# Attention and mixture of experts on one core: transposes as 64-row tiles on two PSUM banks, products with v in four pieces, a new order of steps, one condition at the end

## The chip, the core and the metric

The kernel runs on one core of a Trainium2 chip. Its time is the device time in microseconds (us) of one execution: 1096.68 us, the median of three runs (1095.84 to 1097.83).

## What is computed

Attention with a bias that depends on position, then a mixture of experts with one expert per token (top 1). B = 8, 8 heads, 576 positions, 64 per head; 4608 tokens of width 512; 8 experts with an inner width of 1024.

```python
scores = scale * np.matmul(q, k.transpose(0, 1, 3, 2))
...                                    # bias[head, i, j] from positions, a small two-layer net
scores = scores + bias.transpose(2, 0, 1)[None, :, :, :]
attn = np.exp(scores - np.max(scores, axis=-1, keepdims=True))
attn = attn / (np.sum(attn, axis=-1, keepdims=True) + 1e-09)
attn_out = np.matmul(attn, v)
x = np.ascontiguousarray(attn_out.transpose(0, 2, 1, 3)).reshape(B * S, H * D)
logits = x @ w_gate + modality_bias[modality_id]
e_idx = np.argmax(logits, axis=1)
...                                    # gate_w: softmax of logits at e_idx
for e in range(E):
    mask = e_idx == e
    h = np.maximum(x[mask] @ w1[e], 0.0)
    out[mask] = gate_w[mask, None] * (h @ w2[e])
```

## The kernel before, in words

The kernel has four stretches: a setup (bias tables, first loads), attention, the MoE tiles, and a short end. All instructions are issued in the order in which the program writes them; no scheduler reorders them, and each engine works through its own queue.

**Attention** goes by pairs of heads, n = 0 to 31, four pairs (NP) a batch. A pair has 576 positions in five chunks of rows: 0 to 3 of 128 positions for each of the two heads, and chunk 4, which holds the last 64 positions of both heads side by side. Its steps, by the letter that they have in the table `ORDER` (L560), are:
- P: `prep` (L377) transposes q (P0), k (P1) and their last 64 positions (P2) on TensorE, with an identity as the other operand. H: `high` (ACT) rounds the result to fp32r, with q scaled; G: `low` (DVE) makes the difference from it. Scores are then three products: high by high, high by low, low by high.
- S0 to S4: `scores` (L401) multiplies a chunk of q with k in halves of 288 columns, the two heads on the two 64-row tiles of TensorE, into the banks `sps`; `biased` adds the bias and takes the minimum on DVE (L433). E0 to E4: `exps` (L447), exp with the sum of the row on ACT.
- T0 to T3: `etrans` (L459) transposes a chunk of the exponentials as 64-row tiles, upper rows into bank `eps0`, lower rows into `eps1`; t copies the two banks out. T4 takes chunk 4 as four full 128x128 transposes into one bank.
- C0 to C3: `compact` (L449) gathers on POOL columns 512 to 575 of the exponentials into `rem`; R: `rtrans` (L482) transposes these, four full transposes. C4: two POOL copies (L454) put chunk 4's last columns into the two diagonal blocks of `r4`; N: `rtrans4` (L491) multiplies `r4` by a doubled identity.
- A, B: `av` (L499), the product of the exponentials with v, in two pieces of 256 and 320 columns, the heads on two column tiles; a and b copy the pieces to `xTb`.
- L, V: loads of q, k and v. D, Z: a store and a scatter of routing, on SP and POOL. X, B (without n): one routing step of the batch before, from the lists of `route_steps`; the scatters `s_scatter` (L868) write token numbers into the table `tab` in DRAM, five a batch.

A plus or a minus in the table means the next or the previous pair. The five strings are five slots of a pair's time; `attention` (L568) runs them for n = 0 to 32.

**Routing** of a batch works beside the next batch's attention: logits (`s_logits`), their transposes, the choice of expert, ranks, positions in the table, and the token rows (`s_rows`), which are transposed by TensorE (25 full transposes a batch, logits included), scaled by POOL (L851) and stored.

**The MoE part** goes by tiles of 256 tokens of one expert. Five first tiles use what is known early, then tiles up to number 14 always run, and four more ran here under a condition each: `more` (L1319) loads column 3 of the table `tab_big` on every engine and skips the rest at zero. After them come two more conditions: `small`, tiles of 128 (`tab_small`), and `tiny`, tiles of 32 (`tab_tiny`). None of these had anything left to do here. The values are read by `values_load` in `reg` (L1080) and compared by each engine's queue.

Of the kernel before, what the change touches and what calls it, by code (L numbers as in the profile page):

```python
# [109 lines left out]
class Attn:  # L110
# [155 lines left out]
    def attn_early(self, st, rst):  # L266
# [29 lines left out]
        self.r4 = [cp.tile([P, P], F32, name=f"r4{k}") for k in range(2)]  # L296
        for t in self.r4:
            nc.gpsimd.memset(t, 0.0)
        self.id2 = cp.tile([P, 64], F32, name="id2")
        nc.vector.tensor_copy(self.id2[0:64, :], self.idf[0:64, 0:64])  # L300
        nc.vector.tensor_copy(self.id2[64:P, :], self.idf[64:P, 64:P])
        self.qraw, self.kraw, self.vmain, self.E, self.rem, self.sums, self.xT = {}, {}, {}, {}, {}, {}, {}

    def attn_late(self, st):
# [3 lines left out]
        self.eps = [pp.tile([P, 512], F32, name=f"eps{k}") for k in range(2)]  # L308

    def xbank(self):  # L310
        if "p2" in self.at:
            return self.ring("p2")
        self.n_x += 1
        return self.xps[self.n_x % 2]

    ON_ACT = ("av0", "av1", "e0", "e4", "xr", "lt0")

    def take(self, what, out, ps):

        if what in self.ON_ACT:  # L320
# [128 lines left out]
    def compact(self, n, c):  # L449

        if c == 4:
# [47 lines left out]
    def av(self, n, half):  # L499
# [19 lines left out]
        if half == 1:  # L519
            del self.vmain[n]  # L520
# [1038 lines left out]
```

## Time and profile before

| | |
|---|---|
| median of three runs | 1096.68 us (1095.84 to 1097.83) |
| the profiled execution | 1097.01 us, span of the trace 1095.2 us |
| busy share of the span | PE 94%, PEld (weight loads) 73%, DVE 68%, ACT 62%, POOL 21% |
| attention, steady part | 137.07 to 609.50 us |
| MoE tiles | 629.27 to 1081.40 us |
| after the last product | 1081.40 to 1095.20 us |

Times in the trace count from the start of the span. The profiled execution took 1.8 us more than its span and 0.33 us more than the median. In the rows, `PE` is TensorE's matmuls, `PEld` its weight loads, `PEldq` and `POOLq` the queues' own instructions (loads of values, branches). `L410` is line 410 of the kernel.

### The profile page before, as it was taken

What the parts mean: (1) busy time and instruction counts of PE and PEld (TensorE: products, weight loads), DVE (VectorE), ACT (ScalarE), POOL (GpSimd) and SP (SyncE); (2) the same over time, 40 slices, a digit from 0 to 9 for tenths busy, and PEclk for the clock granted to TensorE, in tenths of its full rate; (3) what the DMA queues carried; (4) which work ended last, traced back from release to release, by engine and by line L of the source; (5) the groups of instructions that cost most, each with busy time, mean ns of one, the idle gap of its engine ahead of it and who ended that gap; (6) DMA issues with size and microseconds to landing.
All of it is one profiled execution on the core that took longest, in us unless ns stands there. A gap on an engine that the chain in (4) does not pass through costs nothing. (4 is left out here: it accounts for less than half of the span.)

```text
span 1095.2 us, 25162 instructions
## 1 busy us (share of the span) xinstructions
PE 1028.3 (94%) x9502; PEld 800.6 (73%) x9502; DVE 739.5 (68%) x1641; ACT 681.5 (62%) x1351; POOL 232.4 (21%) x453
## 2 busy tenths in 40 slices
PE   6989999799999999999999899999999999999994
PEld 3447776566767667677666588889878799889994
DVE  7977778567777677877788466885545455564553
ACT  6767777657768677687776654555534455554552
POOL 0001212222313123142231422431111112111210
PEclk9999999989999999999999999999999999999998
DMA  6853222322322323233234401222545611111110
GB/s 167 213 146 71 66 56 54 74 60 53 90 66 80 65 55 76 71 84 71 53 88 132 122 21 49 59 73 76 182 159 207 206 40 59 39 49 40 64 44 26
DMA packets 125662, 93.29 MB, mean 85 GB/s; under 512 B 94738, under 2 KB 103314, under 8 KB 125525
## 3 DMA queue, kind: packets, MB, share of 16 engines
q1 hardware_dynamic: 117908, 71.20, 23.9%
q0 software_dynamic: 7520, 20.30, 6.1%
q8 instruction: 82, 1.34, 0.6%
q14 instruction: 56, 0.45, 0.2%
q10 hardware_dynamic: 96, 0.00, 0.0%
HBM read 141.40 MB, written 19.38 MB: 147 GB/s over the span
## 5 line engine op out<-in xcount | busy, mean ns | idle before, releaser
L447 ACT ACTIVATE Eb<-Eb,mn 128x576 f32<-128x576 f32 x288 | 221.1, 770 | 50.4 <-DVE mn L433 49.4
L433 DVE CUSTOM_DVE_ANT_0 Eb<-sps,NBm 128x576 f32<-128x576 f32 x256 | 183.5, 754 | 20.7 <-PE sps L410 15.3
L1180 PE MATMUL p<-QK,w1hi 128*128 128x256 f32 x1152 | 163.6, 285 | 1.5 <-ACT w1hi L1153 1.5
L1180 PEld LDWEIGHTS p<-QK,w1hi 128*128 128x128 f32 x1152 | 149.9, 193 | 8.9 <-issue 5.0
L410 PE MATMUL sps<-QK 64*128 64x288 f32 x1536 | 137.9, 309 | 4.7 <-DVE mn L433 4.1
L510 PE MATMUL xps<-eT,vraw 128*64 128x320 f32 (+1 forms) x1024 | 138.4, 412 | 0.0
L323 DVE COPY eT<-eps 128x512 f32<-128x512 f32 x128 | 87.8, 686 | 73.1 <-PE eps L473 73.0
L1183 DVE SCALAR_TENSOR_TENSOR hl<-p,hh 128x512 fp32r<-128x512 f32 x72 | 49.6, 689 | 121.4 <-ACT hh L1182 115.3
L321 ACT COPY eT<-eps 128x512 f32<-128x512 f32 x160 | 92.7, 580 | 53.0 <-PE eps L465 26.2
L1182 ACT ACTIVATE hh<-p 128x512 fp32r<-128x512 f32 x72 | 43.0, 597 | 125.7 <-PE p L1180 105.6
L410 PEld LDWEIGHTS sps<-QK 64*128 64x128 f32 x1536 | 110.3, 188 | 8.6 <-DVE mn L433 7.9
L510 PEld LDWEIGHTS xps<-eT,vraw 128*64 128x64 f32 x1024 | 67.9, 137 | 48.6 <-issue 6.1
L473 PEld LDWEIGHTS eps<-idf,Eb 64*128 64x128 f32 x2048 | 77.9, 139 | 32.9 <-ACT xTb L321 9.9
L1147 DVE TENSOR_TENSOR w2lo<-NBm,w2hi 128x1024 fp32r<-128x1024 f32 x72 | 89.3, 1240 | 15.1 <-ACT w2hi L1146 14.8
L473 PE MATMUL eps<-idf,Eb 64*128 64x64 f32 x2048 | 98.3, 231 | 1.0 <-ACT eT L321 0.6
L1206 POOL DMA_INDIRECT out<-mo,idt x36 | 36.2, 1004 | 296.5 <-ACT mo L1205 279.0
L457 POOL COPY rem<-Eb 128x128 f32<-128x128 f32 x128 | 36.8, 293 | 291.3 <-ACT Eb L447 289.1
L1180 PE MATMUL p<-QK,w1lo 128*128 128x256 f32 x576 | 93.6, 285 | 0.7 <-DVE w1lo L1154 0.7
L1147 DVE TENSOR_TENSOR w1lo<-NBm,w1hi 128x1024 fp32r<-128x1024 f32 x72 | 84.9, 1221 | 3.6 <-ACT w1hi L1146 1.0
L1180 PEld LDWEIGHTS p<-QK,w1lo 128*128 128x128 f32 x576 | 80.2, 194 | 1.1 <-DVE w1lo L1154 1.1
L1146 ACT CAST w2hi<-NBm 128x1024 fp32r<-128x1024 f32 x72 | 74.8, 1039 | 0.0
L1146 ACT CAST w1hi<-NBm 128x1024 fp32r<-128x1024 f32 x72 | 72.3, 1060 | 0.0
(241 smaller groups left out, 1763.2 us busy)
## 6 DMA issues: line engine op xcount, KB each, us to landing
NBm<-moe_w SPq DMA_DIRECT2D x20, 2048.0 KB
NBm<-moe_w SPq DMA_DIRECT2D x40, 1024.0 KB
NBm<-moe_w SPq DMA_DIRECT2D x32, 512.0 KB
NBm<-xTb SPq DMA_DIRECT2D x32, 288.0 KB
qraw<-q SPq DMA_DIRECT2D x64, 128.0 KB
kraw<-k SPq DMA_DIRECT2D x64, 128.0 KB
vraw<-v SPq DMA_DIRECT2D x32, 256.0 KB
xg<-xrb SPq DMA_DIRECT2D x28, 258.0 KB
```

The costliest lines, as they stand in the source:

```text
L321: self.nc.scalar.copy(out, ps)
L323: self.nc.vector.tensor_copy(out, ps)
L410: nc.tensor.matmul(self.sps[h or 0][:, half, 0:HS], QD[:, a, :] if h is None else QK[o, 0, a, P * c : P * c + P], QK[o, 1, b, ks], start=i ...
L433: nc.vector.tensor_tensor_reduce(out=e.rearrange("p (t w) -> p t w", t=2), in0=ps, in1=nb.rearrange("p (t w) -> p t w", t=2), scale=1.0, s ...
L447: self.nc.scalar.activation(e, e, AF.Exp, bias=mn, scale=-1.0, accum_out=sm)
L473: nc.tensor.transpose(self.eps[r][:, w : w + 64], e[o, h, P * k : P * k + P], self.idf[o, o])
L510: nc.tensor.matmul(ps[o, :], v[:, h, k, :] if k < 4 else self.vrem[n % 2][:, o], eT[:, h, k, sl] if k < 4 else rT[:, sl], start=k == 0, st ...
L1146: self.nc.scalar.copy(h, w)
L1147: self.nc.vector.tensor_tensor(l, w, h.bitcast(F32), op=ALU.subtract)
L1180: nc.tensor.matmul(ps[:, a, :], w[:, c, fs], x[:, c, :], start=i == 0, stop=i == len(ops) - 1)
L1182: nc.scalar.activation(hh[:, sl, :], ps, AF.Relu)
L1183: nc.vector.scalar_tensor_tensor(hl[:, sl, :], ps, 0.0, hh[:, sl, :].bitcast(F32), op0=ALU.max, op1=ALU.subtract)
```

## The change

Transposes. A new helper `turn` transposes 128 rows as two 64-row tiles: rows 0 to 63 into bank 0, rows 64 to 127 into bank 1 of a pair of banks (`e` = `eps`, `x` = `xps`). The transposes of q, k and their remainders, of chunk 4, of the remainder columns, and of routing's logits and token rows use it, and every result is copied out as two halves, one per bank. N multiplies E directly, on two column tiles, without `r4` and the copies of C4. GpSimd scales q in advance (`scale_q`, 128x512 in place), so `high` and `low` of q need no scale.

Products with v. `av` works in four pieces of 128, 144, 160 and 144 columns, each in an `eps` bank of its own.

Order. The table becomes the one below, a pair's work reaches two pairs on, and loops go to n_pair + 2. After the colon stands the pair of banks or the bank (`:e`, `:x`, `:e0`) or the engine of a copy (`:a` ACT, `:v` DVE); x and y copy a routing step's result out, O is a routing step without TensorE's banks. E now stands for one head's exp at a time.

End. The big table gets a column 4, which says whether any work of any kind is left. Each conditional tile is preceded by that condition and then by its own; small and tiny lie inside the last of them.

```diff
-        self.r4 = [cp.tile([P, P], F32, name=f"r4{k}") for k in range(2)]
...
+    def turn(self, ps, col, x, idf=None):
+
+        for r in range(2):
+            o = slice(64 * r, 64 * r + 64)
+            n = x.shape[1]
+            self.nc.tensor.transpose(ps[r][0:n, col : col + 64], x[o, :], self.idf[o, o])
...
+    def scale_q(self, n):
+
+        x = self.qraw[n].rearrange("p c h d -> p (c h d)")
+        self.nc.gpsimd.tensor_scalar(x, x, self.SC, None, op0=ALU.mult)
...
-                nc.tensor.transpose(ps[:, j, :], x[:, j, :, :].rearrange("p h d -> p (h d)"), self.idf)
...
+                self.turn(bk, 64 * j, x[:, j, :, :].rearrange("p h d -> p (h d)"))
+            hi, lo = (QK[:, part, a, 0:512].rearrange("p (j r w) -> p j r w", j=4, r=2) for a in range(2))
+            return [
+                (bk[r][:, 0:256].rearrange("p (j w) -> p j w", j=4), hi[:, :, r], lo[:, :, r], 1.0) for r in range(2)
+            ]
...
-                self.nc.gpsimd.tensor_copy(self.r4[n % 2][o, o], self.E[n, 4][o, 0, 512:S])
...
+                for k in range(4):
+                    self.nc.tensor.transpose(bk[h][:, 64 * k : 64 * k + 64], e[o, 0, P * k : P * k + P], self.idf[o, o])
...
+        for c in range(4):
+            self.turn(bk, 256 + 64 * c, self.rem.pop((n, c)).rearrange("p h w -> p (h w)"))
...
-        self.nc.tensor.matmul(ps, self.r4[n % 2], self.id2, start=True, stop=True)
...
+            self.nc.tensor.matmul(
+                ps[o, :],
+                self.E[n, 4][:, 0, 512:S],
+                self.idf[:, o],
+                start=True,
+                stop=True,
+                tile_position=(0, 64 * h),
...
-    CUT = 256
...
+    CUT = (0, 128, 272, 432, S)
...
+        sl = slice(self.CUT[part], self.CUT[part + 1])
+        ps = self.banks[u[0]][int(u[1])][:, 0 : sl.stop - sl.start]
...
     ORDER = (
-        "T2- t2- S0 T4- N- t4- R- P0+ E0 n- r- C0 D",
-        "T3- t3- S1 H0+ G0+ A- E1 L++ C1 a- X B Z",
-        "T0 t0 S2 P2+ P1+ H2+ G2+ H1+ E2 S4 G1+ X D E4 C4 C2 B",
-        "T1 t1 S3",
-        "B- E3 C3 b- X D V+ B Z",
+        "T2-:e t2- S0 Q+ A2--:e0 a2--:a Y:e1 y X:x E0 T3-:e",
+        "x t3- S1 A3--:e0 N-:e1 E0 E1 n- D E1 a3--:v T4-:x R-:x T0:e C0 C1 Z r-:a O",
+        "t4-:a t0 S2 O A0-:e1 a0-:a E2 P2+:x E2 P0+:x",
+        "H2+ T1:e H0+ V t1 S3 E3 D C2 G0+ A1-:e1",
+        "L++ a1-:v E3 S4 P1+:x H1+ G1+ G2+ O Z C3 O E4",
     )
...
-        for n in range(n_pair + 1):
+        for n in range(n_pair + 2):
...
         def more(t):
-            if t < T:
-                with tc.If(self.reg("big", t - K, 3, mybir.ALL_ENGINES, 1) > 0):
+            with tc.If(self.reg("big", t - K, 4, every, 1) > 0):
+                if t == T:
+                    small(0)
+                    with tc.If(self.reg("tiny", NQ, 3, every, 1) > 0):
...
+                with tc.If(self.reg("big", t - K, 3, every, 1) > 0):
                     self.moe_load(t + 1)
                     self.tile(t)
-                    more(t + 1)
+                more(t + 1)
...
         more(self.sure)
-        small(0)
-        with tc.If(self.reg("tiny", NQ, 3, mybir.ALL_ENGINES, 1) > 0):
-            for _ in self.tiny(1):
-                pass
```

What moves, as the two programs have their instructions in their queues (line, operation, out<-in, shape; in brackets the queues and engines for whose semaphores a row waits).

TensorE, around the next pair's k, before: `kraw` is transposed (P1), then come S4 (`QK,QD`), T1, S3, a piece of the product with v, T2, and S0 (the scores that read the other `QK`).

```order
L386 MATMUL xps_77<-idf,kraw_1299 128x128 [waits DMAHW2_49,DMAHW1_49]
L386 MATMUL xps_77<-idf,kraw_1299 128x128 x3
L410 MATMUL sps_728<-QK_73,QD_109 128x288 [waits DVE_49]
L410 MATMUL sps_728<-QK_73,QD_109 128x288 x5
L473 MATMUL eps_730<-idf,Eb 128x64 [waits Activation_49]
...
L410 MATMUL sps_728<-QK_73 128x288 [waits DVE_49]
...
L510 MATMUL xps_78<-eT_105,vraw_1185 64x320 x8
L510 MATMUL xps_78<-rT,vrem_110 64x320 x2
L473 MATMUL eps_730<-idf,Eb 128x64 [waits Activation_49]
...
L410 MATMUL sps_728<-QK_72 128x288 [waits DVE_49]
L410 MATMUL sps_729<-QK_72 128x288 [waits DVE_49]
```

TensorE, the same place, after:

```order
L416 MATMUL sps_738<-QK_72,QD_108 128x288 [waits DVE_49]
L416 MATMUL sps_738<-QK_72,QD_108 128x288 x5
L322 MATMUL xps_77<-idf,kraw_1765 128x64 [waits DMAHW5_49,DMAHW4_49,DVE_49]
...
L322 MATMUL eps_740<-idf,Eb 128x64 [waits Activation_49]
L322 MATMUL eps_741<-idf,Eb 128x64 [waits DVE_49]
...
L416 MATMUL sps_738<-QK_73 128x288 [waits DVE_49,Activation_49]
...
L416 MATMUL sps_738<-QK_73 128x288 [waits DVE_49]
...
L528 MATMUL eps_740<-eT_106,vraw_1723 64x160 [waits Activation_49]
L528 MATMUL eps_740<-eT_106,vraw_1723 64x160 x7
L528 MATMUL eps_740<-rT,vrem_114 64x160 x2
L322 MATMUL eps_740<-idf,Eb 128x64 [waits Activation_49]
```

Now k's transposes follow S4, T2 alone stands between them and S0, and S0 waits for ACT and DVE at its first product, and for DVE at its third (shown) and ninth: high parts, low parts, low part of k's remainder. The third piece of the product with v is in `eps_740`, and T3 behind it waits for ACT to copy that bank out.

DVE between S4 and S0 after the change (L439 with `mn_8` is chunk 4's bias and minimum, with `mn_0` that of S0; L341 and L343 are low parts, L329 the copy t2):

```order
L439 ISA Eb,mn_8_3283<-sps_738,NBr 128x576 [waits DVE_49,PE_49,Pool_49]
...
L341 TENSOR_TENSOR QK_73<-xps_77,QK_73 128x4x64 [waits Activation_49]
L341 TENSOR_TENSOR QK_73<-xps_78,QK_73 128x4x64 [waits Activation_49]
L343 SCALAR_TENSOR_TENSOR QD_109<-xps_77,QD_109 128x64
L343 SCALAR_TENSOR_TENSOR QD_109<-xps_78,QD_109 128x64
L341 TENSOR_TENSOR QK_73<-xps_77,QK_73 128x64
L329 COPY eT_105<-eps_741 128x8x64 [waits PE_49]
L439 ISA Eb,mn_0_3335<-sps_738,NBm 128x576 [waits DVE_49,PE_49,Pool_49]
```

The low parts of k stand behind chunk 4's minimum, and ahead of the copy of T2.

POOL, around a scatter (L868, later L922, a DMA into `tab`), before:

```order
L868 DMA tab<-ids,pos_2532 36992x1 [waits DVE_49]
L851 TENSOR_TENSOR xrb_92<-xrb_92,rec 128x512 [waits Activation_49]
L854 COPY xrb_92<-gt_2403 128x4
L454 COPY r_119<-Eb 64x64 [waits Activation_49]
L454 COPY r_119<-Eb 64x64 [waits DMASW0_49,Pool_49]
L457 COPY rem_2_2603<-Eb 128x128 [waits PE_49,Pool_49]
```

and after:

```order
L458 COPY rem_2_3555<-Eb 128x128 [waits PE_49,Activation_49]
L922 DMA tab<-ids,pos_3161 36992x1 [waits DMASW1_49]
L458 COPY rem_3_3605<-Eb 128x128 [waits Activation_49]
L386 TENSOR_SCALAR qraw_3569<-qraw_3569 128x512 [waits DMAHW2_49,DMAHW1_49]
L798 COPY rec<-mv_3485 64x4 [waits DMAHW5_49]
L458 COPY rem_0_3763<-Eb 128x128 [waits Activation_49]
```

The copies into `r_118` and `r_119` (the two `r4`), one of which waited for a scatter's DMA queue, are gone; a scatter now waits for an earlier scatter, and the scaling of q (L386) has come to POOL.

## Rows read from the trace of the kernel before

**Rows 1.** Busy time by stretch: the stretch and its length in us, then the busy time of PE (its matmuls), PEld (its weight loads), DVE, ACT and POOL with the count of instructions, the granted clock of PE as a share of full speed, the busy share of the DMA engines, and GB/s. The stretches are attention from pair 4 to the last pair's chunk 4, the MoE tiles, and the end.

```profile
137.07:609.50 472.43, 442.14 (x5081) 322.03 (x5082) 350.53 (x992) 342.18 (x826) 117.02 (x292) 0.99 0.30 75
629.27:1081.40 452.13, 449.34 (x2919) 394.02 (x2919) 274.51 (x373) 227.35 (x300) 92.31 (x97) 1.00 0.26 84
1081.40:1095.20 13.80, 0.01 (x1) 0.00 (x0) 0.00 (x0) 0.69 (x1) 1.00 (x1) 0.63 0.09 29
```

**Rows 2.** PE's timeline at the starts of chunk 4's scores (step S4, once a pair): start and length in us, engine, line, operation, out<-in, tile and shape, count.

```profile
137.07 1.07 PE L410 MATMUL sps<-QK,QD 128*128 128x288 f32 x6
205.40 1.06 PE L410 MATMUL sps<-QK,QD 128*128 128x288 f32 x6
231.33 1.06 PE L410 MATMUL sps<-QK,QD 128*128 128x288 f32 x6
282.43 1.06 PE L410 MATMUL sps<-QK,QD 128*128 128x288 f32 x6
349.96 1.06 PE L410 MATMUL sps<-QK,QD 128*128 128x288 f32 x6
370.37 1.05 PE L410 MATMUL sps<-QK,QD 128*128 128x288 f32 x6
556.51 1.06 PE L410 MATMUL sps<-QK,QD 128*128 128x288 f32 x6
574.95 1.06 PE L410 MATMUL sps<-QK,QD 128*128 128x288 f32 x6
```

**Rows 3.** PE's timeline through one pair without routing beside it, same columns: k's transposes, S4, the second piece of the product with v, T2, S0, T4, N, R, P0, T3, and later the first piece and T0.

```profile
121.04 0.60 PE L386 MATMUL xps<-idf,kraw 128*128 128x128 f32 x4
121.66 1.06 PE L410 MATMUL sps<-QK,QD 128*128 128x288 f32 x6
...
124.66 2.38 PE L510 MATMUL xps<-eT,vraw 128*64 128x320 f32 x16
126.87 0.71 PE L510 MATMUL xps<-rT,vrem 128*64 128x320 f32 x4
127.50 0.71 PE L473 MATMUL eps<-idf,Eb 64*128 64x64 f32 x16
128.03 1.03 PE L410 MATMUL sps<-QK 64*128 64x288 f32 x12
128.99 0.66 PE L465 MATMUL eps<-idf,Eb 128*128 128x128 f32 x4
129.48 0.33 PE L494 MATMUL eps<-id,r 128*128 128x64 f32 x2
129.65 0.61 PE L488 MATMUL xps<-idf,rem 128*128 128x128 f32 x4
130.10 0.60 PE L386 MATMUL xps<-idf,qraw 128*128 128x128 f32 x4
130.63 0.89 PE L473 MATMUL eps<-idf,Eb 64*128 64x64 f32 x15
...
132.35 1.95 PE L510 MATMUL xps<-eT,vraw 128*64 128x256 f32 x16
134.13 0.60 PE L510 MATMUL xps<-rT,vrem 128*64 128x256 f32 x4
134.66 0.71 PE L473 MATMUL eps<-idf,Eb 64*128 64x64 f32 x16
```

**Rows 4.** Waits on the `r4` copies, by engine and line: what waited and for what, us in total, times, longest. The first row is PE's in the stretch 100 to 600 us, the second POOL's in the whole execution.

```profile
PE eps L494 <- POOL r L454: 12.0, 3, 7.8
...
POOL r L454 <- DMA tab<-ids,pos: 49.5, 17, 8.1
```

**Rows 5.** Groups of instructions by line and shape: engine, operation, out<-in with shapes, count, then busy us in total and mean ns of one, then idle time before them. The bias and minimum of the scores, the exp, the high and low parts of q and k in two sizes, one copy of a piece of the product with v, and the scaling of token rows on POOL.

```profile
L433 DVE CUSTOM_DVE_ANT_0 Eb<-sps,NBm 128x576 f32<-128x576 f32 x256 | 183.5, 754 | 20.7 <-PE sps L410 15.3
L447 ACT ACTIVATE Eb<-Eb,mn 128x576 f32<-128x576 f32 x288 | 221.1, 770 | 50.4 <-DVE mn L433 49.4
L335 DVE TENSOR_TENSOR QK<-xps,QK 128x512 fp32r<-128x512 f32 x32 | 22.0, 686 | 1.4 <-ACT QK L328 1.4
L335 DVE TENSOR_TENSOR QK<-eps,QK 128x64 fp32r<-128x64 f32 x31 | 6.7, 215 | 0.0
L328 ACT CAST QK<-xps 128x512 fp32r<-128x512 f32 x32 | 18.8, 588 | 1.9
L328 ACT CAST QK<-eps 128x64 fp32r<-128x64 f32 x31 | 6.4, 207 | 0.0
L321 ACT COPY xTb<-xps 128x256 f32<-128x256 f32 x32 | 11.2, 351 | 1.8 <-PE xps L844 1.8
L851 POOL TENSOR_TENSOR xrb<-xrb,rec 128x512 f32<-128x512 f32 x28 | 29.1, 1039 | 28.0 <-ACT xrb L321 27.9
```

**Rows 6.** Loads of the conditions' values by the engines' queues from 1050 us on (line, queue, table, count: shortest/median/longest ns, start of the first and the last), and below them, from the timeline, the last products.

```profile
L1081 PEldq TENSOR_LOAD <-tab_big x2: 300/304/308, 1053.6 to 1077.2; - x2
L1081 PEldq TENSOR_LOAD <-tab_small x1: 308/308/308, 1084.5 to 1084.5; - x1
L1081 PEldq TENSOR_LOAD <-tab_tiny x1: 309/309/309, 1089.6 to 1089.6; - x1
L1081 POOLq TENSOR_LOAD <-tab_small x1: 296/296/296, 1088.5 to 1088.5; - x1
...
1079.44 1.98 PE L1197 MATMUL p<-w2lo,hh 128*128 128x512 f32 x8
```

More of the change, by code (lines that the diff above doesn't have):

```diff
@@ L313, in xbank, with hold, copy @@
         self.n_x += 1
+        assert not any(part[0] == "x" for held in self.held.values() for part in held)
         return self.xps[self.n_x % 2]
-    ON_ACT = ("av0", "av1", "e0", "e4", "xr", "lt0")
-    def take(self, what, out, ps):
-        if what in self.ON_ACT:
+    def hold(self, key, parts):
+        assert not any(part in held for held in self.held.values() for part in parts), (key, parts, self.held)
+        self.held[key] = parts
+    def turn(self, ps, col, x, idf=None):
[3 more added lines that the diff above has]
+            self.nc.tensor.transpose(ps[r][0:n, col : col + 64], x[o, :], self.idf[o, o])
+    def copy(self, by, out, ps):
+        if by == 0:
             self.nc.scalar.copy(out, ps)
@@ L449, in compact, with etrans @@
     def compact(self, n, c):
+        self.rem[n, c] = t = self.raw.tile([P, 2, 64], F32, tag="rem", name=f"rem{n}_{c}", bufs=5)
+        self.nc.gpsimd.tensor_copy(t, self.E[n, c][:, :, 512:S])
+    def etrans(self, n, c, u):
+        e, eT, bk = self.E[n, c], self.eTs[n % 2], self.banks[u]
         if c == 4:
@@ new lines, in rtrans4 @@
+    def rtrans4(self, n, u):
+        ps = self.banks[u[0]][int(u[1])][:, 320:384]
+        for h in range(2):
+            o = slice(64 * h, 64 * h + 64)
+            self.nc.tensor.matmul(
[5 more added lines that the diff above has]
+                tile_position=(0, 64 * h),
+                skip_group_check=True,
+            )
+        return lambda by=0: self.copy(by, self.rT[:, 512:S], ps)
@@ L518, in av @@
                 )
-        if half == 1:
+        if part == 3:
             del self.vmain[n]
-        return lambda: self.take(f"av{half}", self.xT[n][:, sl], ps)
+        dst = self.xT[n][:, sl]
+        return lambda by=0: self.copy(by, dst, ps)
     def first_steps(self, route):
@@ new lines, in start, with end, low @@
+        def start(k, n, *a):
+            f, parts = steps[k]
+            self.hold((k, n, *a[:-1]), parts(a[-1], *a[:-1]))
+            evac[(k, n, *a[:-1])] = f(n, *a)
+        def end(k, n, *a):
+            a, by = (a[:-1], ["av".index(a[-1])]) if a and isinstance(a[-1], str) else (a, [])
+            evac.pop((k, n, *a))(*by)
+            del self.held[k, n, *a]
+        def low(n, k):
+            for x in evac.pop(("P", n, k)):
+                self.low(*x)
+            del self.held["P", n, k]
@@ L592, in attention @@
+            "G": low,
+            "Q": self.scale_q,
+            "V": lambda n: n in self.vmain or self.load_v(n),
             "L": self.load_qk,
         }
-        for k, f in steps.items():
-            pair[k] = lambda n, *a, k=k, f=f: evac.update({(k, n, *a): f(n, *a)})
-            pair[k.lower()] = lambda n, *a, k=k: evac.pop((k, n, *a))()
-        for n in range(n_pair + 1):
+        for k in steps:
+            pair[k] = lambda *a, k=k: start(k, *a)
+            pair[k.lower()] = lambda *a, k=k: end(k, *a)
@@ L1077, in last_tables @@
         tiny = self.table("tiny", ev["nt"], ev["start"])
-        return [s_count] + small + [s_big] + big + [s_tiny] + tiny
+        return [s_count] + small + [s_tiny] + tiny + [s_big] + big
     def reg(self, nm, t, col, engines, hi):
```

307 lines of the change are left out of this document (162 added, 145 removed).

## Prediction, made before the changed kernel ran

> **What bounds the kernel now.** I read the stretches by engine first. From 137.07 to 609.50 us, attention in its steady course, TensorE (PE) is busy 442 of 472 us, ACT 342 and DVE 351; in the MoE part, 629 to 1081, PE is busy 449 of 452; the last 13.8 us hold almost no work [rows 1]. So PE's instruction stream sets the time, and a change pays where it shortens that stream, fills PE's idle time, or cuts the end. PE's clock is full throughout [rows 1]. The MoE tiles stay as they are, so three places are left: the attention pair (one pair of heads of a batch), the stalls between pairs, the end.
>
> The starts of chunk 4's scores, once a pair, give the period. A pair without routing beside it takes 15.41 us (121.66 to 137.07); with it, 282.43 to 349.96 over four pairs gives 16.88 [rows 2, 3]. Three periods are outliers: 25.93, 20.41 and 18.44, so 9.1, 3.5 and 1.6 over 16.88, 14.2 together [rows 2]. Their cause is in the waits: PE stood 12.0 us in three waits for POOL's copies into `r4`, and POOL stood in front of such copies for a DMA of the routing table `tab` [rows 4]. In program order the copies stand behind a scatter.
>
> **A pair's stream on PE.** I take costs from start to start in one pair [rows 3]: 16 transposes of 64 rows 0.53 us (127.50 to 128.03), so two that run side by side on the two row tiles take 65 ns; four full 128x128 transposes 0.45 (remainder, 129.65 to 130.10) or 0.53 (q, 130.10 to 130.63), 112 to 132 ns each; chunk 4's four 0.49; the last remainder 0.17; the two remainders of q and k half of q's, 0.27; the two pieces of the product with v 2.31 and 2.84 (132.35 to 134.66, 124.66 to 127.50).
> - q and k (P0, P1), remainder (R) and P2 as 64-row pairs: four pairs at 65 ns are 0.26. Saved: 0.27 for q, 0.27 for k (its 0.62 to the next start also holds a wait, so I charge it like q), 0.19 for R, 0.11 for P2. Bounds: nothing, if the halves don't overlap in the new places, to 0.27 + 0.36 + 0.19 + 0.14.
> - Chunk 4 (T4): four of one row tile, then four of the other. If they overlap 0.26, if not 0.52; I take 0.46, since neighbours in the queue sit on the same tile. N becomes two products on column tiles, about 0.25 (0.17 to 0.33), with no copies on POOL ahead of them.
> - The product with v in four pieces: the 16 products of 256 columns spread over 1.78 us (132.35 to 134.13), those of 320 over 2.21, so 0.223 and 0.276 a pair of column tiles: 0.84 ns a column and 7.5 ns fixed. Pieces of 128, 144, 160 and 144 columns cost ten pairs each, 1.15 + 1.285 + 1.42 + 1.285 = 5.14, and four ends of about 0.08: 5.47 against 5.15, so +0.32 (bounds +0.2 to +0.6).
> The sum: -0.27 - 0.27 - 0.19 - 0.11 - 0.03 + 0.08 + 0.32 = -0.47, from 14.56 to 14.1 us of PE work a pair.
>
> The rows show no fixed cost that a 64-wide product can't get under when it has a neighbour on the other row tile. The Trainium skill (TensorEngine Tiling (Array Packing), section Instruction Overhead) advises against taking a tiling factor from a dimension that is already small, because each product carries an overhead of about 60 cycles; by that the halved products would save nothing. The 65 ns a pair that the trace shows for the exponentials' transposes speaks against it; the third rival prices it.
>
> **What the new order makes wait.** Before, the next pair's k was transposed at 121.04 and its first scores (S0) came at 128.03, behind S4, T1, S3, a piece of the product with v and T2 [rows 3]. Now k's transposes (P1) come after this pair's S4, and only one group of transposes (T2, 0.53 us) lies between them and S0. From S4's end DVE does the bias and minimum of chunk 4 (0.75 [rows 5]); then both halves of the low part, which needs ACT's casts first. A copy of 64 columns takes 0.21, of 512 0.59 (ACT) or 0.69 (DVE) [rows 5], so 256 about 0.37 and 0.42. DVE: 0.05 + 0.75 + 2 x 0.42 + three small ones of 0.21 = 2.27 us after S4, before the second half of S0's products, which needs the last of these. PE has P1 0.26, T2 0.53 and S0's first half 0.49 by then: 1.0 us of waiting, inside S0. Bounds: 0.2, if DVE has done chunk 4 early and only the casts count (2 x 0.37 - 0.53), to 1.4, with a copy of 0.35 more ahead on DVE. A second wait: T3 uses the bank in which the piece A2 was just made, so ACT must copy A2 out first, some 0.35, behind an exp of 0.77 [rows 5] now and then: 0.5 (0 to 0.9). T1 after A0 in the same way about 0.15. A remainder of idle time, now 15.41 - 14.56 = 0.85, falls to about 0.25, since the exps are issued one head at a time. **A pair without routing: 14.1 + 1.0 + 0.5 + 0.15 + 0.25 = 16.0**, 0.6 more than now (bounds 14.9 to 16.8).
>
> With routing there is 16.88 - 15.41 = 1.47 us more a pair. A batch's 25 full transposes of tokens and logits halve: 25 x 0.056 / 4 = -0.35 a pair; and routing steps now stand in exactly the two gaps (before T3, before E0), filling about 0.45 of them. So 16.0 + 1.47 - 0.35 - 0.45 = 16.67, 0.2 less than now. ACT and DVE stay under PE: each gets a copy's fixed cost more per split bank, 0.15 by the two sizes, some six a pair, 0.9 us, on engines that are busy 72 to 74% [rows 1].
>
> Five pairs have no routing beside them: +3.0. 26 have: -5.5. The pipeline is a step longer (loops to n_pair + 2), so that in the last step copies and exps are not covered by scores: four exposed chains of an exp and a copy of half a bank, 4 x 1.1, say +4 (0 to +8).
>
> **The stalls.** The copies into `r4` are gone from POOL, and N reads E itself. What still waits for a scatter on POOL is the next scatter; behind it the remainder's compaction and the scaling of q, both used half a pair or more later. A scatter has some 8 us until the next one; the wait before went up to 8.1 us behind two scatters [rows 4]. So the stalls go: **-14.2**. Scaling q is new on POOL, about 1.04 us a pair by the nearest POOL row [rows 5]; the loads come a pair ahead, so nothing waits for it, except perhaps once at the start (+0.5, 0 to +1).
>
> **The end.** PE's queue loads the small tiles' condition at 1084.5, the tiny one's at 1089.6, and the span ends at 1095.2: two steps of 5.1 and 5.6 us, in which no work runs [rows 6]. Now one condition (column 4 of the big table) skips both: the end is at 1084.5 + 5.6 = 1090.1 for PE, and POOL, whose load for the small tiles is at 1088.5, is free about then. **-5** (0, if POOL's last transfer sets the end anyway, to -6). The four conditional tiles each take one load and one branch more; PE's queue runs ahead of its products there: it loads the last condition of the big table at 1077.2, while the products end at 1081.4 [rows 6], so most of it is hidden: +2 (0 to +5).
>
> **Sum** against the profiled execution of 1097.01 us (span 1095.2), 0.3 above the median of 1096.68: 3.0 - 5.5 + 4 - 14.2 + 0.5 - 5 + 2 = -15.2, so 1081.8; to the median 1081.5.
>
> **Rivals.**
> 1. *The wait in S0 eats the gain (slower).* One mechanism: S4, DVE's minimum, casts, low parts, S0. With its upper bound, and A2's copy behind an exp each time, a pair gains 0.4 + 0.3 = 0.7 us: 31 x 0.7 = +22, so 1103. It decides from +0.5 a pair (+15.5) on. For it: DVE has seven steps in that stretch and PE one group of transposes. Against it: routing steps fill gaps in 26 pairs. The Trainium skill (same page, Gotcha 1: PSUM Pressure) says that different row tiles write to different banks and that software must keep them in step; each step here holds two banks, which is the wait at T3, and no run shows more of it yet.
> 2. *The gaps are smaller.* If DVE reaches the low parts early (0.4 instead of 1.0) and A2's copy comes at once, a pair gains nothing beyond the PE sum: 31 x -0.65 = -20, so 1061. For it: the split exps make ACT free sooner.
> 3. *Halved products cost as much as full ones.* Then 0.84 a pair and 0.28 of routing come back; half of it falls into the waits: 31 x 0.6 to 31 x 1.1, so 1100 to 1116, say 1109. Against it: the 65 ns.
> 4. *The stalls stay*, because a scatter lands later than the next is due and the compaction behind it is late for R: +14, so 1095. For it: landings in this trace hold POOL up to 8.1 us, about the time between scatters.
>
> **How the numbers follow.** Forecast 0.48 (1072 to 1092), rival 1 0.20 (1094 to 1112), rival 2 0.18 (1052 to 1070), rival 3 0.04, rival 4 0.10 (1089 to 1101). The likeliest gives 1081.5. The range 1060 to 1104 leaves out about half of rival 2, a third of rival 1 and rival 3: 0.19. A measurement of this kernel can tell about 0.2% (2.2 us) from no change. Faster: 0.48 + 0.18 + 0.04 of rival 4 = 0.70; same: 0.02 of rival 1 + 0.05 of rival 4 = 0.07; slower: 0.18 + 0.04 + 0.01 = 0.23.
>
> **What would show it.** Right: periods near 16.0 without routing and 16.7 with; no outlier of 20 us; no wait of PE for POOL; S0's products idle about 1 us behind DVE's low part; T3 behind ACT's copy of A2; remainder and q transposes near 0.26 us; the product's pieces 1.2 to 1.5 us; one table load of PE's queue after the last tile, and an end 5 us shorter. Wrong: periods above 16.5 without routing, halved transposes at 0.5 us, PE or POOL idle behind a scatter, or a last step that grows by over 8 us.

## The result and the profile after

The changed kernel took 1112.22 us (median of four runs, 1108.42 to 1116.1) against 1096.26 us before (four runs on the same chip): 1.0149 times as long, 95% interval 1.0116 to 1.0183. The forecast was 1081.5 us, 1060 to 1104. So on this chip the change made the kernel 1.5% slower, and the range missed it; on another chip (below) the ratio was 1.0039, with an interval that holds 1. Ratios and intervals leave out runs more than 1.5% above the fastest of the same kernel, in the changed kernel's second set two of ten, the profiled one of 1117.65 us among them.

The profiled execution after took 1111.95 us with a span of 1110.2. Its stretches, in the columns of [rows 1] (length, busy time of PE, PEld, DVE, ACT and POOL, granted clock, share of the DMA engines, GB/s): attention from the first to the last start of S4, the MoE tiles from their first product to the last, and the end.

```profile
78.13:613.26 535.13, 486.30 (x7746) 413.11 (x7746) 402.41 (x1224) 393.18 (x1158) 157.81 (x294) 0.96 0.32 76
632.41:1100.78 468.37, 453.68 (x2944) 396.41 (x2944) 275.11 (x380) 226.87 (x301) 94.18 (x97) 0.99 0.25 80
1100.78:1110.20 9.42, 0.00 (x0) 0.00 (x0) 0.00 (x0) 0.69 (x1) 1.00 (x1) 0.72 0.09 33
```

By the same marks the kernel before has this row for attention:

```profile
76.80:609.50 532.70, 500.06 (x5775) 365.29 (x5774) 396.49 (x1104) 389.44 (x943) 127.30 (x325) 0.99 0.30 75
```

It had 76.80 us to the first S4, then 532.70, a tail of 19.77 to the first MoE product, 452.15 of MoE tiles and 13.78 of end [rows 1, 2, 6]. After: 78.13, 535.13, 19.15, 468.37, 9.42. So attention is 2.4 us longer where it was to gain, the MoE tiles are 16.2 longer where nothing was forecast, and the end is 4.4 shorter. The granted clock is 0.96 and 0.99 in the two long stretches, where [rows 1] have 0.99 and 1.00.

**Attention.** PE's timeline at starts of S4, to be read as [rows 2]:

```profile
123.09 1.06 PE L416 MATMUL sps<-QK,QD 128*128 128x288 f32 x6
...
138.29 1.06 PE L416 MATMUL sps<-QK,QD 128*128 128x288 f32 x6
...
216.74 1.06 PE L416 MATMUL sps<-QK,QD 128*128 128x288 f32 x6
...
242.07 1.06 PE L416 MATMUL sps<-QK,QD 128*128 128x288 f32 x6
...
257.83 1.06 PE L416 MATMUL sps<-QK,QD 128*128 128x288 f32 x6
...
273.33 1.06 PE L416 MATMUL sps<-QK,QD 128*128 128x288 f32 x6
...
288.54 1.05 PE L416 MATMUL sps<-QK,QD 128*128 128x288 f32 x6
```

A pair without routing now takes 15.20 us (123.09 to 138.29; 15.41 before). With routing, 15.76, 15.50 and 15.21 follow one another from 242.07 on, where 16.4 to 17.5 stood. But 216.74 to 242.07 is 25.33 us. Such a pair stands in every batch from the second on: 25.33, 24.58, 25.11, 23.51, 23.19 and 23.46; only the first batch's pair at this place had 16.79. Over that value the six are 44.4 us longer, and without them the new order would have won 42.0 us in attention. With the forecast's 14.2 for the old stalls, 27.8 of them are in the pairs; only the 42.0 is measured.

**The long pair, link by link.** PE, as in [rows 3], stands 5.9 us in front of N, for DVE:

```profile
225.38 1.20 PE L528 MATMUL eps<-eT,vraw 128*64 128x144 f32 x16
...
232.71 0.48 PE L504 MATMUL eps<-idf,Eb 128*64 128x64 f32 x4 [5.88 <-DVE eT L329]
```

DVE is late with its copy t3 because a product of routing (L814, the transposed logits times the reciprocals `rec`) stands ahead of it and waits for POOL:

```profile
223.12 0.23 DVE L329 COPY lt<-eps 128x64 f32<-128x64 f32 x1 [1.17 <-PE eps L790]
231.50 0.56 DVE L814 TENSOR_TENSOR lw<-xps,rec 128x160 f32<-128x160 f32 x2 [8.15 <-POOL rec L798]
231.97 0.68 DVE L329 COPY eT<-eps 128x512 f32<-128x512 f32 x1
```

POOL's copy into `rec` (L798, 0.18 us) stands behind the scaling of q, and that waits for its data:

```profile
222.15 0.31 POOL L458 COPY rem<-Eb 128x128 f32<-128x128 f32 x1
229.84 1.49 POOL L386 TENSOR_SCALAR qraw<-qraw 128x512 f32<-128x512 f32 x1 [7.38 <-DMA qraw<-q]
231.29 0.18 POOL L798 COPY rec<-mv 64x4 f32<-64x4 f32 x1
```

SP issued these loads late. Its queue had stood for a transfer of 1 KB, `mv`, which POOL prepares when routing begins; v's and q's loads come behind it:

```profile
214.97 0.49 SPq L780 DMA_DIRECT2D mv<-mv  x1
215.56 0.53 SPq L372 DMA_DIRECT2D vraw<-v  x1
...
217.36 1.26 SPq L359 DMA_DIRECT2D qraw<-q  x2
```

In a pair without that transfer q's loads go out earlier against S4 (257.83):

```profile
253.85 1.26 SPq L359 DMA_DIRECT2D qraw<-q  x2
```

That is 4.0 us before S4, and there POOL begins the scaling at 259.62, 5.8 us after the issue, without a wait. In the long pair the issue is 0.6 us after S4, and the data are not there until 229.8, 12.5 us after the issue and 7.4 us after POOL was free for them. Against S4 the data are at least 11.3 us later than in the other pair: 4.6 of that come from the late issue, and at least 6.7 from a slower landing, whose cause no run shows.

That q's load stands behind `mv` is not new. In the kernel before it did too, but there no scaling on POOL waited for it, and SP stood for `mv` 15.8 us in five waits (100 to 600 us), at most 6.6:

```profile
222.12 0.49 SPq L740 DMA_DIRECT2D mv<-mv  x1
222.67 1.26 SPq L353 DMA_DIRECT2D qraw<-q  x2
```

The waits in sum (what waited for what, us, times, longest; PE, DVE and SP from 100 to 600 us, POOL in the whole execution):

```profile
PE eps L504 <- DVE eT L329: 24.7, 6, 5.9
...
DVE lw L814 <- POOL rec L798: 38.3, 6, 8.2
...
POOL qraw L386 <- DMA qraw<-q: 75.3, 9, 19.3
...
SPq L780 <- POOL mv L778: 36.7, 6, 11.8
```

Of POOL's nine waits two, 25.2 us, are at the start of the kernel, and seven, 50.1, in the steady part. Six waits of DVE for `rec` make 38.3 us and six of PE at N 24.7; the six long pairs cost 44.4. The clock makes up most of the difference. In slices of 0.2 us the granted clock is at its lower level (1.2 instead of 2.4 GHz) from 231.1 to 237.9: it falls while PE still waits and is back 5.2 us after N began. In the mean of the long pair it is 0.87, and PE is busy 18.46 us where the first batch's pair at this place has 15.84 (columns as in [rows 1]); over the six pairs that is 17.1 us more busy time:

```profile
153.50:170.29 16.79, 15.84 (x266) 13.15 (x264) 13.39 (x41) 12.85 (x38) 2.79 (x6) 1.00 0.42 98
216.74:242.07 25.33, 18.46 (x265) 15.18 (x263) 13.12 (x41) 12.84 (x38) 4.76 (x8) 0.87 0.53 72
```

**A pair that nothing disturbs** (columns as in [rows 3]; S4, P1, T2, S0, A2, T3, A3, N, T4, R, T0):

```profile
107.91 1.06 PE L416 MATMUL sps<-QK,QD 128*128 128x288 f32 x6
108.89 0.47 PE L322 MATMUL xps<-idf,kraw 64*128 64x64 f32 x8
109.20 0.66 PE L322 MATMUL eps<-idf,Eb 64*128 64x64 f32 x16
110.09 1.46 PE L416 MATMUL sps<-QK 64*128 64x288 f32 x12 [0.24 <-ACT QK L334]
111.48 1.31 PE L528 MATMUL eps<-eT,vraw 128*64 128x160 f32 x16
...
113.45 0.71 PE L322 MATMUL eps<-idf,Eb 64*128 64x64 f32 x16 [0.39 <-ACT xTb L327]
...
114.94 1.20 PE L528 MATMUL eps<-eT,vraw 128*64 128x144 f32 x16
...
116.21 0.28 PE L504 MATMUL eps<-idf,Eb 128*64 128x64 f32 x4
116.43 0.47 PE L467 MATMUL xps<-idf,Eb 64*128 64x64 f32 x8
116.73 0.42 PE L322 MATMUL xps<-idf,rem 64*128 64x64 f32 x8
116.98 0.69 PE L322 MATMUL eps<-idf,Eb 64*128 64x64 f32 x16
```

The halved transposes cost what was worked out: P1 0.31 us (108.89 to 109.20), N 0.22, T4 0.30, R 0.25. The pieces cost 1.58 (without the wait), 1.27, 1.25 and 1.37 us, 5.47 together. S0 begins 0.36 us late and takes 1.39 instead of 0.98; T3 waits 0.39 for A2's copy.

**MoE.** The first tile takes 30.0 us (28.4 before), the second and third 33.3 and 33.2 (25.0 and 26.5 before), the fourth 24.1 (24.7), all later ones within 0.03 us of before. In the first, PE waits for routing's product `lw` (L814), in the second and third for the copies of routing's token rows, among others:

```profile
656.02 1.09 PE L1247 MATMUL xps<-idf,NBr 128*128 128x128 f32 x8 [3.64 <-DVE lw L814]
...
688.65 0.80 PE L1283 MATMUL xps<-w2hi,hh 128*128 128x512 f32 x1 [1.47 <-ACT NBm L327]
...
709.87 0.50 PE L1283 MATMUL xps<-w2hi,hh 128*128 128x512 f32 x1 [1.30 <-DVE NBm L329]
...
721.03 0.79 PE L1283 MATMUL xps<-w2hi,hh 128*128 128x512 f32 x1 [2.37 <-DVE NBm L329]
721.62 0.63 PE L1283 MATMUL xps<-w2hi,hl 128*128 128x512 f32 x1
```

The output of these products is an `xps` bank that a routing step holds until both of its halves are read, and at 688.21 ACT's half stands behind 2 us of casts:

```profile
686.31 2.02 ACT L1232 CAST w1hi<-NBm 128x1024 fp32r<-128x1024 f32 x2
688.21 0.40 ACT L327 COPY NBm<-xps 128x256 f32<-128x256 f32 x1
```

The second product at 721.62 shows the other part of the price: 0.63 us where 0.39 is usual, with the granted clock at half. The two tiles together, columns as in [rows 1]:

```profile
662.42:728.90 66.48, 55.66 (x339) 48.44 (x338) 42.72 (x100) 25.73 (x37) 19.61 (x22) 0.90 0.18 49
```

**The end.** Queue loads from 1040 us on, as in [rows 6]: there is one last load on PE's queue, at 1096.9, and on POOL's at 1103.1, and no small or tiny table behind.

```profile
L1167 PEldq TENSOR_LOAD <-tab_big x5: 296/564/574, 1049.6 to 1096.9; - x5
L1167 POOLq TENSOR_LOAD <-tab_big x5: 284/284/294, 1054.6 to 1103.1; - x5
```

### The profile page after: what moved, and what is told of

Same layout as the page of the kernel before. It is cut to its first block, busy times and chain, and to the rows that moved or that the text cites. A ratio compares the mean times of both kernels' runs of the same rounds, so it can differ in the third digit from the quotient of the medians.

```text
span 1110.2 us, 30041 instructions
## 1 busy us (share of the span) xinstructions
PE 1018.1 (92%) x11590; PEld 853.6 (77%) x11590; DVE 748.0 (67%) x1777; ACT 683.5 (62%) x1576; POOL 266.3 (24%) x419
## 5 line engine op out<-in xcount | busy, mean ns | idle before, releaser
L453 ACT ACTIVATE Eb<-Eb,mn 128x576 f32<-128x576 f32 x288 | 224.6, 787 | 46.0 <-DVE mn L439 45.8
L439 DVE CUSTOM_DVE_ANT_0 Eb<-sps,NBm 128x576 f32<-128x576 f32 x256 | 183.5, 754 | 21.0 <-PE sps L416 15.3
L416 PE MATMUL sps<-QK 64*128 64x288 f32 x1536 | 153.9, 319 | 11.7 <-ACT QK L334 6.0
L528 PE MATMUL eps<-eT,vraw 128*64 128x144 f32 (+2 forms) x2048 | 158.3, 298 | 6.6 <-ACT eT L327 5.7
L528 PEld LDWEIGHTS eps<-eT,vraw 128*64 128x64 f32 x2048 | 123.3, 140 | 31.9 <-ACT eT L327 16.6
L416 PEld LDWEIGHTS sps<-QK 64*128 64x128 f32 x1536 | 118.2, 193 | 24.7 <-DVE QK L341 10.0
L329 DVE COPY eT<-eps 128x512 f32<-128x512 f32 x128 | 87.8, 686 | 49.5 <-PE eps L322 45.7
L1233 DVE TENSOR_TENSOR w2lo<-NBm,w2hi 128x1024 fp32r<-128x1024 f32 x72 | 89.3, 1240 | 16.2 <-ACT w2hi L1232 16.1
L322 PE MATMUL eps<-idf,Eb 64*128 64x64 f32 x2048 | 94.8, 230 | 4.8 <-ACT xTb L327 1.8
L1283 PE MATMUL xps<-w2hi,hh 128*128 128x512 f32 x208 | 86.6, 416 | 7.3 <-DVE NBm L329 3.7
L322 PEld LDWEIGHTS eps<-idf,Eb 64*128 64x128 f32 x2048 | 81.8, 143 | 9.8 <-ACT xTb L327 4.3
L1283 PE MATMUL xps<-w2hi,hl 128*128 128x512 f32 x208 | 84.3, 405 | 0.0
L327 ACT COPY eT<-eps 128x512 f32<-128x512 f32 x128 | 77.4, 605 | 4.6 <-PE eps L322 2.1
```

The costliest lines, as they stand in the source:

```text
L322: self.nc.tensor.transpose(ps[r][0:n, col : col + 64], x[o, :], self.idf[o, o])
L327: self.nc.scalar.copy(out, ps)
L329: self.nc.vector.tensor_copy(out, ps)
L416: nc.tensor.matmul(self.sps[h or 0][:, half, 0:HS], QD[:, a, :] if h is None else QK[o, 0, a, P * c : P * c + P], QK[o, 1, b, ks], start=i ...
L439: nc.vector.tensor_tensor_reduce(out=e.rearrange("p (t w) -> p t w", t=2), in0=ps, in1=nb.rearrange("p (t w) -> p t w", t=2), scale=1.0, s ...
L453: self.nc.scalar.activation(e, e, AF.Exp, bias=mn, scale=-1.0, accum_out=sm)
```

## The experiments

Ratios are to the kernel before on the same chip, with 95% intervals; there it took 1102 to 1105 us, so ratios, not times, are to be compared with the result above. "Steady" and "MoE" are the stretches of each profile by the marks above; what a repair gives back of them is taken against the first chip's profile, so across chips.

| kernel | median us | ratio | steady | MoE |
|---|---|---|---|---|
| changed, first chip | 1112.2 | 1.0149 (1.0116 to 1.0183) | 535.1 | 468.4 |
| changed, again | 1112.4 | 1.0039 (0.9998 to 1.0079) | 540.9 | 467.3 |
| rec on DVE | 1080.6 | 0.9805 (0.9773 to 0.9837) | 510.3 | 461.8 |
| loads earlier | 1086.0 | 0.9848 (0.9811 to 0.9885) | 505.8 | 472.1 |
| mv from POOL's queue | 1089.5 | 0.9879 (0.9838 to 0.9921) | 513.9 | 468.3 |
| scaling of q later | 1101.4 | 1.0000 (0.9969 to 1.0032) | 527.2 | 470.5 |
| pq for the last batch | 1093.0 | 0.9908 (0.9873 to 0.9943) | 531.6 | 452.2 |
| three repairs | 1061.5 | 0.9618 (0.9582 to 0.9654) | 504.3 | 450.3 |
| three, and mv | 1062.1 | 0.9632 (0.9580 to 0.9683) | 504.3 | 450.4 |
| three, and q later | 1079.6 | 0.9814 (0.9753 to 0.9875) | 517.8 | 450.8 |
| before, N direct | 1084.8 | 0.9845 (0.9815 to 0.9875) | 524.3 | 451.2 |
| before, new end | 1097.9 | 0.9958 (0.9928 to 0.9987) | 539.2 | 451.9 |

**The changed kernel again.** 

> The changed kernel itself, on the same chip as the three others of this set, so that their steps can be taken against it: about 1.015 times the kernel before, six long periods of 23 to 25 us, MoE stretch 468 us.

A miss in the ratio: 1.0039, and its interval holds 1, so that the loss of 1.5% is shown on the first chip alone. Its ten runs spread from 1100 to 1118 us. The six long pairs (26.25, 24.70, 24.71, 24.42, 22.64, 25.21) and the MoE stretch were there again.

**rec on DVE.**

```diff
-            nc.gpsimd.tensor_copy(rec[0:64, 4, :].rearrange(...)[:, 1, :], st["mv2"])
+            nc.vector.tensor_copy(rec[0:64, 4, :].rearrange(...)[:, 1, :], st["mv2"])
```

> The changed kernel (1112.2 us), with routing's small copy of mv2 into rec on DVE instead of POOL; everything else as changed. Theory A (POOL's order): in one pair a batch, POOL stands some 7.5 us at the scaling of q for q's late load, the copy into rec stands behind it, DVE's product lw stands 8.2 us behind that copy, and PE's N behind DVE. Then lw no longer waits on POOL, PE's 24.7 us at N go, and only q itself is late for P0 (scaled at 231.3 where P0 would be due near 229), so 2 to 4 us of each 7 to 8.8 us stay: six long periods of 18 to 21 instead of 23 to 25, and 3 to 4 us less in the first MoE tile. 1112 - 30 = 1082 (1070 to 1092). Theory B (the batch's first logits are late by themselves, because mv2 lands late behind the scatters): DVE waits for mv2 instead, the long periods stay at 23 to 25, 1108 to 1113.

The ratio is 0.9805, a little better than theory A's 1082, which is 0.987 of 1096.3; theory B is out. DVE's product no longer waits for POOL at all, only for PE (DVE's waits, 100 to 600 us):

```profile
DVE lw L814 <- PE xps L322: 5.7, 7, 0.9
```

Four of the six long pairs came down to 17 to 21 us. Two of 23 stayed, and 6.5 us went in the MoE stretch: its first tile took 26.3 us instead of 30.0, its second 30.2 instead of 33.3.

**Loads earlier.**

```diff
-        "t4-:a t0 S2 O A0-:e1 a0-:a E2 P2+:x E2 P0+:x",
+        "t4-:a t0 S2 L++ O A0-:e1 a0-:a E2 P2+:x E2 P0+:x",
...
-        "L++ a1-:v E3 S4 P1+:x H1+ G1+ G2+ O Z C3 O E4",
+        "a1-:v E3 S4 P1+:x H1+ G1+ G2+ O Z C3 O E4",
```

> The changed kernel (1112.2 us), with the loads of q and k (L++) in the third slot ahead of the routing step O instead of the fifth; everything else as changed. Theory A: what makes q late is SP's queue, in which the loads stand behind the transfer of mv, which waits for POOL; issued ahead of it, q has landed when POOL comes to the scaling, nothing stands behind it, and the six long periods of 23.2 to 25.3 us come down to about 16.5: 1112 - 46 = 1066 (1060 to 1072), with the granted clock at 0.98 or more. Theory B (scatters and their landing hold POOL, whatever q does): periods above 20 us stay, 1100 or more.

The mechanism holds: POOL's waits at the scaling fell from nine (75.3 us) to two, both in the first 30 us of the kernel:

```profile
POOL qraw L386 <- DMA qraw<-q: 25.5, 2, 19.5
```

The gain was 29 us of steady time, not 46: long pairs of 16.9 to 22.8 us are left, and the MoE stretch, which these loads don't touch, was 472.1 us. The copy into `rec` now waits for `mv` itself, 11.4 us in six waits. Expected was 1066, 0.972 of 1096.3; measured 0.985.

**mv from POOL's queue.**

```diff
-            nc.sync.dma_start(mv2, mv[64:P, :])
+            nc.gpsimd.dma_start(mv2, mv[64:P, :])
```

> The changed kernel, with routing's transfer of mv into mv2 issued from POOL's queue, where mv is made, instead of SP's; everything else as changed. Theory D (SP's queue is the root): in the step in which routing starts, SP stands 6 to 12 us for POOL's mv and all loads of v, q and k come 5 to 8 us late; issued from POOL, the loads go out on time, the scaling of q finds its data, and the long periods of 23 to 25 come to 16.5 to 18: 30 to 45 us less than the changed kernel. Theory A alone (the order on POOL is enough of a cause, the loads would be late anyway from traffic): POOL still waits 6 us or more for q, less than 15 us gained.

Theory D holds in its direction: with SP's queue free of that one transfer the waits at the scaling fell to four, 26.9 us, of which the start has two, 25.4. Steady time is 21 us shorter. The gain by the two ratios, 1.0039 and 0.9879, is 18 us, short of the expected 30 to 45: three pairs of 20 to 22.6 us remain.

**Scaling of q later.**

```diff
-        "T2-:e t2- S0 Q+ A2--:e0 a2--:a Y:e1 y X:x E0 T3-:e",
+        "T2-:e t2- S0 A2--:e0 a2--:a Y:e1 y X:x E0 T3-:e",
...
-        "t4-:a t0 S2 O A0-:e1 a0-:a E2 P2+:x E2 P0+:x",
+        "t4-:a t0 S2 Q+ O A0-:e1 a0-:a E2 P2+:x E2 P0+:x",
```

> The changed kernel, with the scaling of q (Q+) moved from the first slot to the third, behind the routing copy of mv2 into rec on POOL and still ahead of P0; everything else as changed. Theory A (the order on POOL: only what stands behind the scaling suffers): lw no longer waits behind the late q, PE's 22 to 25 us at N go, and P0 waits for the late scaling by 2 to 4 us in six pairs: long periods of 17 to 21, 25 us or more less than the changed kernel, as with the copy on DVE but without its gain in the MoE stretch (468): ratio to the kernel before 0.98 to 0.995. Rival: rec or mv2 is late in any case; ratio above 1.00.

A miss in size: steady time is 8 us shorter where 25 or more were expected. `rec` is freed, but now the scaling stands behind a scatter, and PE's transposes of q wait for it twelve times, pairs that had been undisturbed among them (16.45 instead of 15.2 us):

```profile
PE xps L322 <- POOL qraw L386: 18.1, 12, 6.4
```

**Pq for the last batch.**

```diff
-            if self.route_next(kind, {"X": "x", "Y": "x0"}.get(kind, "")):
+            if self.route_next(kind, {"X": "q", "Y": "q0"}.get(kind, "")):
...
+        self.banks["q"] = self.pq
```

> The changed kernel (1112.2 us), with the last batch's routing steps beside the MoE tiles in the two banks pq, which are idle there, instead of xps, which the tiles' products also use; attention as changed. Theory A: the second and third MoE tile (33.3 and 33.2 us against 25.0 and 26.5 before) are long because a step holds both xps banks until ACT and DVE have copied them out, behind casts and differences of weights of 2 us each, so PE waits for a bank (1.5, 1.3, 2.4, 0.9 us in the trace) and its clock falls to half for 3.4 to 6.8 us after such waits. Then these tiles come back to about 26 us: 1112 - 12 = 1100 (1096 to 1105). Theory C: the loss is in the routing chain itself (DVE's lw behind POOL's copy into rec, behind three scatters): 1108 to 1113.

The MoE stretch is 452.2 us, that of the kernel before (452.15): with idle banks all 16.2 us go, with `rec` still on POOL, and theory A's 12 us were too few. Theory C's time is out, but its chain is in part real: `rec` on DVE alone took 6.5 of the 16.2 us, since a bank is held until L814 has its `rec`. With idle banks the late `rec` cost PE nothing here. The ratio, 0.9908, lies below the expected 0.9997 to 1.0079. Between the two profiles 22 us went: 16.2 here, 3.5 in attention's steady stretch, where the six long pairs stand 35.8 us over 16.79 instead of 44.4, and 2.3 at the start, the tail and the end. The second and third tile take 27.1 and 26.3 us at a full clock (to be read against the 66.48 us above):

```profile
653.23:706.63 53.40, 50.42 (x339) 44.45 (x338) 40.87 (x84) 25.76 (x37) 15.83 (x18) 1.00 0.18 46
```

**Before, with N direct.** The change's `rtrans4` in the kernel before, without the copies of C4.

> The kernel before (1096.3 us), with the last remainder multiplied directly on two column tiles, as in the change, and without POOL's two copies into r4; everything else as before. The prediction's term: PE's waits for POOL's r copies (12.0 us, and 14.2 us in the periods) go, N costs 0.1 us more a pair: 1096.3 - 14.2 + 2 = 1084 (1081 to 1087), no period above 17.6. Rival: what stood behind the scatter on POOL after these copies (the remainder's compaction, used by R at the same place) is late in their place, and the outliers stay: 1094 to 1098.

0.9845, 17 us on this chip (13.8 to 20.4), where 14.2 less 2 were expected. N (L493) waits 0.8 us for DVE's copy of its bank and no longer for POOL (100 to 600 us):

```profile
PE eps L493 <- DVE eT L323: 0.8, 1, 0.8
```

The waits for the copies are gone, but the size of their gain is open. Periods of 18.1, 18.4 and 19.0 us remain where none above 17.6 was expected, and in the profile attention's steady stretch is only 8.4 us shorter than the 532.7 of the kernel before on the first chip. Another 3.6 us of that profile's gain are at the end, 10.2 us instead of 13.8, which this edit does not touch.

**Before, with the new end.** The condition on column 4 and the nesting, alone.

> The kernel before, with the change's end alone: column 4 of the big table and one condition for all that is left, small and tiny inside it. The prediction's terms: -5 at the end (0 to -6) and +2 for the four conditional tiles (0 to +5), so -3; by the traces of the changed kernel (end 9.1 to 9.4 us instead of 13.8, conditional tiles 23.57 instead of 23.55 us) -4.4 us: ratio 0.996. Rival: the additional loads and branches cost what the end saves, ratio 1.000.

0.9958, or 4.6 us (1.4 to 7.9), and 9.0 us after the last product instead of 13.8. The old end took 10.2 us in the profile with N direct, so no one pair of traces gives the size of this gain; the ratio does, within its interval.

**Three repairs together** (rec on DVE, loads earlier, pq):

> The three repairs together: the copy of mv2 into rec on DVE, the loads of q and k ahead of the routing step, and pq for the last batch's routing. If the two causes are separate and their sizes add, attention's steady stretch is 495 to 508 us (535 in the changed kernel) and the MoE stretch 452 (468): 1058 to 1066 where the kernel before takes 1096 to 1103, a ratio of about 0.965. Rival: the first two only swap one wait for another (rec for mv2's own landing), and it is no better than the larger of them with pq, 0.972.

1061.5 us, the fastest of all, 3.8% under the kernel before and, by the two ratios, 47 us under the changed one on the same chip. The stretches, attention and MoE, columns as in [rows 1]:

```profile
76.60:580.92 504.32, 477.22 (x7747) 405.20 (x7747) 405.83 (x1231) 393.38 (x1158) 156.94 (x287) 0.99 0.33 80
598.69:1049.00 450.31, 447.84 (x2944) 392.21 (x2944) 275.26 (x381) 226.89 (x301) 94.63 (x96) 1.00 0.26 84
```

MoE's gain adds in full. Attention's gains overlap: 24.9 us for `rec` alone, 29.4 for the loads alone, 30.8 for both. Five of the six long pairs take 17.0 to 18.6 us, and one of 22.1 is left; there the copy into `rec`, now on DVE, waits for the landing of `mv` itself, which SP had issued at 217.0:

```profile
226.34 0.16 DVE L798 COPY rec<-mv 64x4 f32<-64x4 f32 x1 [4.39 <-DMA mv<-mv]
```

**Three repairs and more.** 

> As the three repairs together, and the transfer of mv on POOL's queue as well. If SP's wait for POOL is what is left of late loads, the long periods come down to 16.5 to 17 and attention's steady stretch to 488 to 498: 1050 to 1060, ratio 0.955 to 0.965. If what is left is slow landing of DMAs at these places, the same as the three repairs alone.

> The three repairs together, and the scaling of q in the third slot as well. If a late q still costs something in the version with three repairs, the steady stretch goes from 504 to 495 or less: ratio 0.955. If what is left there is not q but slow landings and the pair's own waits, it stays at 0.96 to 0.965.

Neither helps. The transfer of `mv` on POOL's queue changes nothing once the loads go ahead of it (steady 504.3 in both). The later scaling costs 13.5 us of steady time again, since it stands behind a scatter.

## Why the prediction was wrong, step by step

- **The scaling of q: the step that failed.** "The loads come a pair ahead, so nothing waits for it" counted the order on PE, not the queues. The load is issued in the last slot and the scaling stands in the first slot of the next step, some 6 us later; on SP's queue the load stands behind `mv`, as it did before the change, and SP's wait for it was not followed; and what stood behind the scaling on POOL was named as the compaction and not the copy into `rec`, which DVE and PE need at once. This cost 44.4 us where 0 to 1 was given (35.8 in the run with `pq`, whose attention is the same). Any one of the links broken (rec, loads, mv) gave back 21 to 29 us of steady time, and with rec and loads together the six pairs stand 8.3 us over 16.79. The scaling itself took 1.49 us, not 1.04, which cost nothing by itself.
- **"The MoE tiles stay as they are": the second one.** The last batch's routing runs beside the first tiles, and its steps took both `xps` banks, into which the tiles' products write. 16.2 us where 0 was given; with idle banks, 0. The Trainium skill (TensorEngine Tiling (Array Packing), Gotcha 1: PSUM Pressure) says that row tiles put more pressure on PSUM, since they write to different banks; this trace agrees, in the stretch where it was not looked for.
- **PE's stream of a pair: right.** 14.1 us forecast; 14.02 by adding the undisturbed pair's starts without its waits, four pieces at 5.47 as forecast. So the third rival fell: halved products side by side cost little more than half, 0.25 us for R against 0.45. The Trainium skill (TensorEngine Tiling (Array Packing), Instruction Overhead) advises against taking a tiling factor from a dimension that is already small; the prediction read this as no saving at all, and the trace does not agree with that reading.
- **The new waits: right place, too large.** 1.0 us in S0 was 0.77, 0.5 at T3 was 0.39, the other 0.4 nothing. A pair without routing took 15.19 instead of 16.0. With routing, the cycle of four with an undisturbed first pair (16.79, 15.76, 15.48, 15.21) gives 15.81 instead of 16.67. That is the second rival's size and a little more: pairs gave -27.8 us, forecast -2.5.
- **The stalls at N: right in place, size open.** With N alone the waits for POOL (12.0 us) are gone from the kernel before; its ratio gives 17 us, its steady stretch 8.4, and -14.2 lies between them. What is less here is more in the pairs: only the sum of both, -42.0, is measured. PE's clock was not full throughout, as the prediction had it: in the two longest of the old stalls (205.40 to 231.33, 349.96 to 370.37) it was 0.87 and 0.92 in the mean.
- **The tail**, +4 forecast, was -0.6; the start +1.3 (+0.5 forecast).
- **The end**, -5, was -4.4 between the two profiles and -4.6 alone, with 1.4 to 7.9 as the interval. The additional branches, +2, cost 0.02 us a tile.

In sum: -27.8 - 14.2 + 44.4 + 1.3 - 0.6 + 16.2 - 4.4 = +14.9 us between the two profiled executions. The fourth rival came near (a stall on POOL behind a late transfer), but with a load of q in place of a scatter, and at three times its price. With both failed steps mended the ratio is 0.9618, which is 1054 of 1096.3, near the second rival's 1061, though by a kernel that nobody had forecast.

**Open:** why `mv`'s 1 KB took until 226.3 after its issue at 217.0, and why one pair of 19.5 to 24 us at the second batch stayed in every repaired version. The kernel before has its longest pair at the second batch too, 25.93 us, and 18.1 and 18.4 with N direct. Traffic at these places is a guess; no run took it away. Two direct tests were not run: the changed kernel with the scaling of q back in `high` and `low`, and its routing steps beside the MoE tiles with one `xps` bank at a time.

## What to carry to other kernels

When an instruction is added to a queue, read what stands behind it there and who waits for that; here 0.18 us of work behind a late load stopped three engines. When a load is moved, follow its own queue back to the last thing that can block it. A step that holds two banks instead of one must be looked up in every place where it runs, not only in the loop that the change is about.

## What the runs showed of the hardware

A wait of some 6 us of PE cost more than itself: the granted clock was at half from 231.1 to 237.9 in the pair shown, 5.2 us of it after the wait. In the second and third MoE tile, where single waits are 0.9 to 2.4 us and follow one another closely, it was 0.90 in the mean over 66.48 us, at half from 678.2 to 681.6, 688.4 to 691.9 and 719.2 to 726.0. A product of 512 columns took 0.63 us there instead of 0.39, and 0.43 instead of 0.23 from start to start. The single wait of 3.64 us in the first tile, between long runs of products, left the clock at full. And in the kernel with three repairs a transfer of 1 KB, issued at 217.0, kept DVE waiting for its landing until 226.3; SP's queue had issued loads of q and k (128 KB each) before it, from 209.9 to 215.6, and those of v and q came behind it from 222.3 on.
